# Q/K stacks loaded by sixteen rows: a new partition order and a second scratch tensor for the last four features

## The chip, the core and the metric

The kernel runs on one core of a Trainium2 chip. Its engines are TensorE (PE; its weight loads are listed apart as PEld), VectorE (DVE), ScalarE (ACT), GpSimd (POOL) and SyncE (SP). In this kernel SP issues all data transfers; 16 DMA engines carry them out. The metric is device time in microseconds of one launch, lower is better. Before the change three runs took 1097.66, 1098.9 and 1102.91 us, so the median is 1098.9 us.

## The reference

One transformer block in float32 on x of 2048 tokens by 640 features: sliding-window attention, then a gated MLP that mixes tokens. Only the first half matters for the change:

```python
B, S, D = x.shape
H = 32; Dh = D // H; W = 256                      # 32 heads of 20 features
qkv = (x @ wqkv).reshape(B, S, 3, H, Dh).transpose(2, 0, 3, 1, 4)
q, k, v = qkv
scores = einsum("bhqd,bhkd->bhqk", q, k) * Dh ** -0.5
mask = (i - j >= 0) & (i - j < W)                 # causal, 256 wide
p = softmax(where(mask, scores, -1e9))
o = einsum("bhqk,bhkd->bhqd", p, v)
h = x + merge_heads(o) @ wo                       # x here is layer-normed before wqkv
h2 = h + gated_mlp(layernorm(h))                  # gelu, token mixing by a 2048 x 2048 matrix, w_out
```

## The kernel before, in words

**Split operands.** Q and K are kept to nearly float32 precision as sums of three bfloat16 parts (part 0 the largest). A score q·k is then a sum of six products of parts: (1,0), (0,1), (0,0), (0,2), (2,0), (1,1) as (Q part, K part). The kernel stacks these six along the contraction: one bfloat16 matmul over 6 x 20 = 120 partitions makes a whole score. Such an operand is called a stack. Three more partitions (120 to 122) carry the row maxima against ones, so that the score comes out with its maximum subtracted.

**Making the parts.** Ten weight tiles m = 0 to 9 of 128 columns give Q and K transposed; tiles 0 to 4 hold the first sixteen heads and 5 to 9 the others, and within five tiles the 640 columns are ordered by (Q or K, feature, head), 8 rows of features by 16 heads in a tile. `qk_item(m, c)` (15 matmuls) makes tile m for 512 tokens (chunk c); `split_qk` turns the result into three bfloat16 parts in a tile `sg` (VectorE, ScalarE and GpSimd in turn; three buffers), and SP stores it to a scratch tensor `qk_d` in HBM with one transfer of 384 KB (L650). Items run in the order n = 0 to 23 (tiles 0 to 5, pairs of tiles, chunks 0 to 3 within a pair), then sixteen "dense" items for tiles 6 to 9 that are mixed into the first scores.

**Loading the stacks.** The heads come in eight groups g of four. `load_stack(g)` (L343) reads a group's rows from `qk_d` into one of three slots: two tiles st[0], st[1] for the first and the second 1024 tokens (b), each with Q and K side by side (a = 0 and 1). For each of the six pairs j it moves the 20 rows of one part to every sixth partition, j, j + 6, ...; 2 x 6 x 2 = 24 transfers of 20 rows by 8 KB. It is a generator: each `next` issues one transfer, and the callers set how many go out at each step.

**Where the loads stand.** All transfers are queued on SP in the order of the program, and SP issues them in that order, each after the waits it needs. Group 0 is loaded during items n = 16 to 21, three transfers an item, and one transfer for each of the first score units; group 1 during the dense items, three each from n = 7. From there on the main loop has steps s = 0 to 129: at step s unit s (a group and a block of 128 keys: scores, exp on ScalarE, masks on GpSimd, product with V) and the maximum pass of unit s + 18 (`max_item`, VectorE). Group g of 2 to 7 is loaded during the sixteen steps from s = 16(g - 2), one or two a step; it is first used by the maximum pass fourteen steps after its first transfer.

**What a transfer waits for.** The compiler gives the transfers eight completion semaphores in rotation (DMAHW0 to DMAHW7 in the listings below), so each transfer on SP waits until the one eight places before it has landed. PE, DVE, ACT and POOL follow the written order as well around these places (L612 to L614 are the matmuls of `qk_item`, L377 the matmuls of the first eighteen maximum units, L373 of the others, L426 the scores, L454 the product with V; L630 to L645 are the steps of `split_qk`; L606 loads a row of scales `std`, L570 a weight tile `wqraw`).

## Time and profile before

| | before |
|---|---|
| median of three runs | 1098.9 us |
| the profiled execution's own time | 1096.99 us |
| its span, first to last instruction | 1095.3 us |
| PE busy | 1073.5 us, 98% |
| DVE, ACT, POOL busy | 779.6, 603.7, 308.9 us |
| data moved | 194.78 MB in 92293 packets |
| granted TensorE clock | 1.000 |

The profile is of one execution. The span lies inside the execution's own time; 1.7 us are around it. The stages that the change touches lie between about 146 us (first load of group 0) and about 410 us (last load of group 7). In a timeline row the first number is the start, the second the length; "SPq" is SP issuing a transfer, whose length is the issue alone and not the movement of the data. "[0.28 <-X]" is idle time of the engine before the row and what ended it; "issue" there means that the engine waited for nothing that the profile shows.

### The profile page before, as it was taken

The page shows a single profiled execution, that of the slowest core. Times are in us where ns is not written, and L with a number is a line of the kernel's source. Part 1 is how long each engine was busy: PE and PEld are TensorE (multiplying, and loading weights), DVE is VectorE, ACT ScalarE, POOL GpSimd, SP SyncE. Part 2 cuts the span into 40 slices and gives each one's busy share as a digit, 9 for nine tenths or more (in the row PEclk, how much of TensorE's full clock was granted, in tenths as well). Part 3 has the DMA queues.
Part 4 walks back from the last instruction along what each step waited for, and adds up shares of the span by engine and source line. Part 5 has one row for each costly group of instructions (what it writes and reads, how often), then busy time and mean ns, then how long its engine had stood idle before and what let it go on. Part 6 is the DMA issues. An engine that isn't in the chain of part 4 may idle for free.

```text
span 1095.3 us, 28703 instructions
## 1 busy us (share of the span) xinstructions
PE 1073.5 (98%) x11045; PEld 967.9 (88%) x11045; DVE 779.6 (71%) x2157; ACT 603.7 (55%) x1257; POOL 308.9 (28%) x446
## 2 busy tenths in 40 slices
PE   8999999999999999999999999999999999999998
PEld 8998886668888787699999998999999899999998
DVE  6643445779999997586677678656556899988674
ACT  4444433249989899766766557433358433333331
POOL 4414445668766677622200012000001000000000
PEclk9999999999999999999999999999999999999999
DMA  7834566465665565679845342242341567684542
GB/s 257 296 117 118 174 212 217 150 214 174 191 186 184 187 192 172 193 217 289 316 179 186 113 135 77 71 142 87 126 150 51 176 230 249 231 280 139 181 156 97
DMA packets 92293, 194.78 MB, mean 178 GB/s; under 512 B 11958, under 2 KB 46278, under 8 KB 88262
## 3 DMA queue, kind: packets, MB, share of 16 engines
q1 hardware_dynamic: 92156, 192.95, 54.0%
q8 instruction: 87, 1.43, 0.5%
q14 instruction: 50, 0.41, 0.1%
HBM read 127.90 MB, written 64.95 MB: 176 GB/s over the span
## 4 chain that ended last, share of the span: by engine, by line
PE 84%; DMA 4%; issue 4%; ACT 3%; DVE 2%; POOL 1%; SPq 1%; ACTq 0%; POOLq 0%; DVEq 0%
PE g L1217 23%; PE zb L1102 8%; PE pv L454 7%; PE bank L373 5%; PE bank L426 5%; PE qk L612 4%; PE qk L613 4%; PE qk L614 4%; PE out_x L1381 3%; PE zx L1042 2%; PE out_v L1381 2%; PE zv L1042 2%; PE zy L1042 1%; PE zw L1042 1%; PE bank L377 1%
## 5 line engine op out<-in xcount | busy, mean ns | idle before, releaser
L429 ACT ACTIVATE pt<-bank 128x384 f32<-128x384 f32 (+1 forms) x452 | 180.5, 486 | 14.5 <-PE bank L426 9.7
L1217 PE MATMUL g<-zl,aw 128*128 128x432 f32 x768 | 168.9, 357 | 1.0 <-ACT zl L864 1.0
L383 DVE CUSTOM_DVE_ANT_0 junk<-bank,strip 128x288 bf16<-128x288 f32 x392 | 155.8, 452 | 9.8 <-PE bank L373 5.6
L864 ACT ACTIVATE aw<-fx 128x512 fp32r<-128x512 f32 (+2 forms) x152 | 86.1, 587 | 128.4 <-DVE fx L858 53.6
L1217 PEld LDWEIGHTS g<-zl,aw 128*128 128x128 f32 x768 | 144.0, 188 | 7.4 <-ACT zl L864 1.4
L858 DVE TENSOR_TENSOR aw<-fx,aw 128x512 fp32r<-128x512 f32 (+2 forms) x152 | 95.7, 638 | 58.8 <-ACT aw L864 53.8
L454 PE MATMUL pv<-pt,v_sb 128*32 128x192 f32 (+3 forms) x1984 | 133.3, 322 | 2.9 <-POOL pt L433 1.2
L1217 PE MATMUL g<-ze,aw 128*128 128x432 f32 x576 | 132.6, 359 | 2.3 <-DVE row L858 2.3
L1217 PEld LDWEIGHTS g<-ze,aw 128*128 128x128 f32 x576 | 107.1, 188 | 9.0 <-DVE row L858 3.7
L433 POOL TENSOR_SCALAR_AFFINE_SELECT pt<-pt 128x512 f32<-128x512 f32 x128 | 82.6, 646 | 58.1 <-ACT pt L429 55.1
L426 PE MATMUL bank<-slot 123*32 123x288 bf16 (+8 forms) x1296 | 94.8, 273 | 1.0 <-ACT pt L429 0.6
L373 PE MATMUL bank<-slot 120*32 120x288 bf16 (+4 forms) x1248 | 91.6, 275 | 3.0 <-issue 2.8
L454 PEld LDWEIGHTS pv<-pt,v_sb 128*32 128x32 f32 x1984 | 64.1, 110 | 10.2 <-POOL pt L433 5.1
L436 POOL TENSOR_SCALAR_AFFINE_SELECT pt<-pt 128x512 f32<-128x512 f32 x112 | 71.0, 634 | 0.0
L426 PEld LDWEIGHTS <-slot 123*32 123x32 bf16 x1728 | 59.3, 96 | 11.5 <-issue 1.7
L858 DVE TENSOR_TENSOR row<-g,row 128x432 f32<-128x432 f32 x80 | 48.3, 603 | 21.3 <-PE g L1217 20.9
L373 PEld LDWEIGHTS <-slot 120*32 120x32 bf16 x1408 | 51.0, 95 | 14.0 <-issue 5.6
L383 DVE CUSTOM_DVE_ANT_0 junk<-bank,mask 128x384 bf16<-128x384 f32 (+2 forms) x120 | 51.4, 444 | 16.6 <-PE bank L377 14.7
L645 POOL TENSOR_TENSOR sg<-rest,sg 128x512 bf16<-128x512 f32 x39 | 45.6, 1169 | 57.7 <-ACT sg L644 45.2
L630 DVE TENSOR_TENSOR rest<-qk,std 128x512 f32<-128x512 f32 x36 | 24.8, 690 | 42.4 <-PE qk L614 41.2
L635 ACT ACTIVATE sg<-rest 128x512 bf16<-128x512 f32 x39 | 24.6, 631 | 54.1 <-DVE rest L630 52.3
L118 PE MATMUL wo_ps<-xb,xb 128*128 128x320 f32 x260 | 52.4, 311 | 0.5 <-DVE mvc L1496 0.5
(289 smaller groups left out, 2534.5 us busy)
## 6 DMA issues: line engine op xcount, KB each, us to landing
slot<-qk_d SPq DMA_DIRECT2D x144, 160.0 KB
fx<-wsp_in SPq DMA_DIRECT2D x32, 512.0 KB
qk_d<-sg SPq DMA_DIRECT2D x39, 384.0 KB
o_d<-ot SPq DMA_DIRECT2D x64, 128.0 KB
xb<-qk_d SPq DMA_DIRECT2D x48, 160.0 KB
fx<-hn_d SPq DMA_DIRECT2D x24, 320.0 KB
z_d<-row SPq DMA_DIRECT2D x16, 432.0 KB
g_d<-row SPq DMA_DIRECT2D x16, 432.0 KB
```

Source lines behind the costliest of these rows:

```text
L373: nc.tensor.matmul(ps[32 * j:32 * j + 32, o:o + w], one(st, 120, 0, hh, q0, 32), k, start=True, stop=True, tile_position=(0, 32 * j))
L383: nc.vector.tensor_tensor_reduce(out=junk[:, :n], in0=ps[:, :n], in1=keep, scale=1.0, scalar=NEG, op0=OP.add, op1=OP.max, accum_out=m_cols ...
L426: nc.tensor.matmul(ps[32 * i:32 * i + 32, b + o:b + o + w], one(st, 123, 1, hh, k0, 32), q, start=True, stop=True, tile_position=(0, 32 * i))
L429: nc.scalar.activation(pt[:, hh, :n], ps[:, :n], AF.Exp, scale=SCALE)
L433: nc.gpsimd.affine_select(out=pt[:, :, :P], in_=pt[:, :, :P], pattern=[[0, 4], [1, P]], base=0, channel_multiplier=-1, compare_op=OP.is_ge ...
L436: nc.gpsimd.affine_select(out=pt[:, :, 256:], in_=pt[:, :, 256:], pattern=[[0, 4], [-1, P]], base=-1, channel_multiplier=1, compare_op=OP. ...
L454: nc.tensor.matmul(ps[32 * hh:32 * hh + 32, a - 512 * c:b - 512 * c], v_sb[:, kb, v0:v0 + 32], pt[:, hh, a - kb * P:b - kb * P], start=fir ...
L858: (eng or nc.vector).tensor_tensor(out=out, in0=a, in1=b, op=op)
L864: nc.scalar.activation(out, a, AF.Copy)
L1042: nc.tensor.matmul(ps, a[x], b[:, y], start=start and m + x + y == 0, stop=stop and m == n - 1 and x == 1, skip_group_check=True)
L1102: nc.tensor.matmul(b[0][:, :HF], a[:, x, kk], win2[0][:, y, kk, h * HF:(h + 1) * HF], start=kk + x + y == 0, stop=kk == KD - 1 and x == 1)
L1217: nc.tensor.matmul(ps, w[m][:, x, k], zc[k][m][:, y], start=start and k + x + y == 0, stop=stop and k == 3 and x == 1, skip_group_check=True)
```

## The change

The stacks get another order of partitions. Pair j now lies seven partitions apart, j, j + 7, ..., for the first sixteen features; every seventh row (6, 13, ..., 111) and the last eight rows (112 to 119) hold the last four features, 24 rows of (pair, feature). The host orders the weight columns to match: tiles 0, 1 hold Q and tiles 2, 3 K for features 0 to 15, tile 4 the last four features of Q and then of K (the same for tiles 5 to 9).

`qk_d` keeps the first sixteen features alone. A new scratch tensor `qr_d` holds the last four features already repeated for the six pairs. So tiles 4 and 9 are stored by six transfers a chunk rather than one: for Q and for K, each part goes to all pairs that use it (three, two and one copies; the source is repeated by a zero step). A stack is loaded by 32 transfers rather than 24: 24 of 16 rows, and for each (b, a) one of 16 and one of 8 rows from `qr_d`. The bytes of a stack stay the same; the stores of tiles 4 and 9 double from 384 to 768 KB.

The pace of the generators follows: four loads an item for n = 16 to 22 (28 of the 32 of group 0), with the four from `qr_d` for the first token half last among these; four rather than three for group 1; two a step (three at some early steps of group 2) in the main loop.

```diff
@@ -49,7 +49,9 @@
     const = pool(ctx, "const")
     dram = pool(ctx, "dram", space=DRAM)
 
-    qk_d = dram.tile([2, 3, 2, 2 * DH, H // 2, S // 4], F32, name="qk_d")
+    qk_d = dram.tile([2, 2, 3, 2, 16, H // 2, S // 4], F32, name="qk_d")
+    qr_d = dram.tile([2, 2, 2, 6, DH - 16, H // 2, S // 4], F32, name="qr_d")
+    PAIRS = ((1, 0), (0, 1), (0, 0), (0, 2), (2, 0), (1, 1))
     m_d = dram.tile([8, 2, 3, 32, 64], F32, name="m_d")
     o_d = dram.tile([H, 32, S], F32, name="o_d")
     wo_d = dram.tile([KD, 2, P, D], F32, name="wo_d")
@@ -334,13 +336,19 @@
                 for h, ones in zip(st, slot_w[0]):
                     nc.sync.dma_start(h[120:123, 1], ones[120:123, 1])
                     yield
-            parts = ((0, 0), (0, 1), (0, 2), (1, 0), (1, 1), (2, 0))
-            loads = [(b, j, a) for b in range(2) for j in range(6) for a in range(2)]
+            q, heads = g // 4, slice(g % 4 * 4, g % 4 * 4 + 4)
+            loads = []
+            for b in range(2):
+                for j, parts in enumerate(PAIRS):
+                    for a in range(2):
+                        loads.append((st[b][j:j + 106:7, a], qk_d[q, a, parts[a], b, :, heads]))
+                for a in range(2):
+                    last = qr_d[q, a, b, :, :, heads].rearrange("j d h t -> (j d) h t")
+                    loads += [(st[b][6:112:7, a], last[:16]), (st[b][112:6 * DH, a], last[16:])]
             if g == 0:
-                loads.sort(key=lambda load: load[2])
-            for b, j, a in loads:
-                src = qk_d[g // 4, parts[j][a], b, a * DH:(a + 1) * DH, g % 4 * 4:g % 4 * 4 + 4]
-                nc.sync.dma_start(st[b][j:6 * DH:6, a], src)
+                loads = loads[:12] + loads[16:28] + loads[12:16] + loads[28:]
+            for out, src in loads:
+                nc.sync.dma_start(out, src)
                 yield
 
         def tokens(st, rows, a, hh, t0, n):
@@ -645,10 +653,21 @@
                 nc.gpsimd.tensor_tensor(out=sg[:, 2, :], in0=rest, in1=sg[:, 1, :], op=OP.subtract)
                 if final:
                     yield
-                T = S // 4
-                base = qk_d[m // 5, 0, c // 2, m % 5 * 8, 0, c % 2 * 256:c % 2 * 256 + 256]
-                nc.sync.dma_start(bass.AP(tensor=base.tensor, offset=base.offset,
-                                          ap=[[T, P], [2 * 2 * DH * H // 2 * T, 3], [1, 256]]), sg.bitcast(F32))
+                T, n, part = S // 4, H // 2, sg.bitcast(F32)
+                b, t = c // 2, slice(c % 2 * 256, c % 2 * 256 + 256)
+                if m % 5 < 4:
+                    base = qk_d[m // 5, m % 5 // 2, 0, b, m % 5 % 2 * 8, 0, t]
+                    nc.sync.dma_start(bass.AP(tensor=base.tensor, offset=base.offset,
+                                              ap=[[T, P], [2 * 16 * n * T, 3], [1, 256]]), part)
+                    return
+                for a in range(2):
+                    for p in range(3):
+                        js = [j for j, x in enumerate(PAIRS) if x[a] == p]
+                        base = qr_d[m // 5, a, b, js[0], 0, 0, t]
+                        step = (js[-1] - js[0]) // max(1, len(js) - 1)
+                        nc.sync.dma_start(bass.AP(tensor=base.tensor, offset=base.offset,
+                                                  ap=[[T, 64], [4 * n * T * step, len(js)], [1, 256]]),
+                                          part[64 * a:64 * a + 64, p:p + 1].to_broadcast([64, len(js), 256]))
 
             halves = [slice(0, HD), slice(HD, D)]
             load_x(0)
@@ -746,9 +765,9 @@
                     load_wqk(2 * q + 4 + r % 2)
                 for _ in qk_item(2 * q + r % 2, r // 2):
                     pass
-                if 16 <= n < 22:
-                    for _ in range(3):
-                        next(ld0, None)
+                if 16 <= n < 23:
+                    for _ in range(4):
+                        next(ld0)
 
             def dense_tail():
                 split_wqk(8)
@@ -762,7 +781,7 @@
                         s1 = pool(x01, "slot1p", side="right")
                         add_slot(1, [s1.tile([P, 2 * S], F32R, name=f"slot1_{i}") for i in range(2)])
                     if n >= 7:
-                        for _ in range(3):
+                        for _ in range(4):
                             next(ld1, None)
 
             pool_order.enter_context(tc.manual_schedule(engines={mybir.EngineType.Pool}))
@@ -787,8 +806,9 @@
         early, pre_ps = None, []
         for s in range(NU + 2):
             if s % NT == 0 and s < 6 * NT:
+                assert s == 0 or next(ld, 0) == 0
                 ld = load_stack(s // NT + 2)
-            for _ in range(1 + s % 2 if s >= NT else 2 * (s > 1)):
+            for _ in range(2 if s >= NT else (2 + (s % 2 == 0 and s < 14)) * (s > 1)):
                 next(ld, None)
             u1 = s + LEAD
             if s in (3, 4, 7, 10, 12):
@@ -1584,7 +1604,9 @@
     c = np.ascontiguousarray
     x = np.asarray(A_x)[0]
     w = np.asarray(A_wqkv).reshape(D, 3, H, DH)
-    wqk = w[:, :2].reshape(D, 2, 2, H // 2, DH).transpose(2, 1, 4, 0, 3).reshape(2 * D // P, 8, KD, P, H // 2)
+    wqk = w[:, :2].reshape(D, 2, 2, H // 2, DH).transpose(2, 1, 4, 0, 3)
+    wqk = np.concatenate([wqk[:, a, d] for d in (slice(0, 16), slice(16, DH)) for a in range(2)], axis=1)
+    wqk = wqk.reshape(2 * D // P, 8, KD, P, H // 2)
     wqk = wqk.transpose(0, 3, 2, 1, 4).reshape(2 * D // P, P, KD, P)
     wv = w[:, 2].reshape(D, D)
     wo = np.asarray(A_wo).reshape(H, KD, 4, D).transpose(1, 2, 0, 3).reshape(D, D)
```

The order of the instructions on PE, DVE, ACT and POOL is the same before and after; SP's changes. The first place is the end of the items n = 20 to 22 on SP, ahead of the first maximum pass. Before (`slot_0_102` is st[0] of group 0, `sg_2` and `sg_3` are chunks 2 and 3, L650 the stores):

```order
L570 DMA wqraw_1597<-wqk_in 128x640
L650 DMA qk_d<-sg_2_1591 128x3x256
L343 DMA slot_0_102<-qk_d 20x2048 x3
L606 DMA std_0_1626<-rstd_d 128x512
L650 DMA qk_d<-sg_2_1620 128x3x256
L650 DMA qk_d<-sg_3_1649 128x3x256
L606 DMA std_1_1684<-rstd_d 128x512
```

The three loads after the store of item 20 are the last that the first maximum pass needs; nothing of the stack stands behind item 21's store. After the change the same place, with the waits (`slot_0_103` is st[0], `slot_1_104` st[1], the lines are those of the new file; the six stores of item 20 begin four rows above):

```order
L668 DMA qr_d<-sg_2_1606 64x2x256 [waits DMAHW6_49]
L668 DMA qr_d<-sg_2_1606 64x256 [waits DMAHW7_49]
L351 DMA slot_1_104<-qk_d 16x2048 [waits DMAHW0_49]
L351 DMA slot_1_104<-qk_d 16x2048 [waits DMAHW1_49]
L351 DMA slot_1_104<-qk_d 16x2048 [waits DMAHW2_49]
L351 DMA slot_1_104<-qk_d 16x2048 [waits DMAHW3_49]
L614 DMA std_0_1648<-rstd_d 128x512 [waits DMAHW4_49,DVE_49]
L660 DMA qk_d<-sg_2_1641 128x3x256 [waits DMAHW5_49,Pool_49]
L351 DMA slot_0_103<-qr_d 16x2048 [waits DMAHW6_49]
L351 DMA slot_0_103<-qr_d 8x2048 [waits DMAHW7_49]
L351 DMA slot_0_103<-qr_d 16x2048 [waits DMAHW0_49]
L351 DMA slot_0_103<-qr_d 8x2048 [waits DMAHW1_49]
```

The last four loads that the first maximum pass needs have moved one item later, behind item 21's store, and each waits for the transfer eight rows above it, two of which are stores of item 20.

The second place is PE at the first maximum pass, the weight load that waits for the stack. Before:

```order
L613 MATMUL qk_0_1710<-xa,wqh_1535 128x512
L614 MATMUL qk_0_1710<-xa,wql_1536 128x512 [waits Pool_49]
L377 LDWEIGHTS slot_0_102 [waits DMAHW5_49,DMAHW4_49,DMAHW6_49,DMAHW2_49,DMAHW7_49,DMAHW1_49,DMAHW0_49]
L377 MATMUL bank_128<-slot_0_102 128x128
L612 MATMUL qk_0_1710<-xa,wqh_1535 128x512
```

`qk_0_1710` is the dense item of tile 7, chunk 0, whose matmuls stand around it. After (L385 and L620 to L622 are L377 and L612 to L614 in the new file):

```order
L621 MATMUL qk_0_1741<-xa,wqh_1544 128x512
L622 MATMUL qk_0_1741<-xa,wql_1545 128x512 [waits Pool_49]
L385 LDWEIGHTS slot_0_103 [waits DMAHW5_49,DMAHW6_49,DMAHW4_49,DMAHW7_49,DMAHW1_49,DMAHW0_49]
L385 MATMUL bank_129<-slot_0_103 128x128 [waits DMAHW1_49]
L620 MATMUL qk_0_1741<-xa,wqh_1544 128x512
```

Its place among PE's instructions has not moved; what it waits for now includes the four loads from `qr_d`, and the matmul itself waits for the last of them.

## The prediction

> **What bounds the kernel now.** I read the page first, then the busy times by stage, then what PE waited for, and last SP's timeline at the places where loads moved. The page and the stages:
>
> ```profile
> span 1095.3 us, 28703 instructions
> PE 1073.5 (98%) x11045; PEld 967.9 (88%) x11045; DVE 779.6 (71%) x2157; ACT 603.7 (55%) x1257; POOL 308.9 (28%) x446
> ```
> ```profile
> 0.00:240.00 240.00, 236.80 (x1263) 192.75 (x1264) 130.22 (x325) 95.07 (x164) 112.37 (x111) 1.00 0.60 196
> 240.00:440.00 200.00, 193.44 (x5823) 163.10 (x5822) 182.93 (x929) 185.47 (x482) 142.89 (x247) 1.00 0.59 183
> 440.00:1095.00 655.00, 643.22 (x3968) 612.04 (x3960) 466.49 (x906) 323.20 (x614) 53.62 (x90) 1.00 0.51 170
> ```
>
> The columns are the stretch, its length, PE, PEld, DVE, ACT and POOL busy, clock, DMA share, GB/s. PE is busy throughout. The change touches 146 to 410 us, and there PE is idle for no more than the 200 − 193.4 = 6.6 us of the attention stage. So a gain has a small ceiling; a loss has none, since every microsecond that PE waits for a stack is added to the end: the instructions of PE follow a written order. What that idle time waited for, from 240 to 440 us (us in total, times, longest):
>
> ```profile
> PE bank L373 <- issue: 3.4, 5, 1.6
> PE pv L454 <- issue: 1.1, 3, 0.6
> PE bank L426 <- ACT pt L429: 0.9, 6, 0.2
> PE bank L426 <- issue: 0.3, 1, 0.3
> ```
>
> Nothing of it is put down to a stack load. 3.4 + 1.1 + 0.3 = 4.8 us have no cause that the profile shows. All transfers go through SP:
>
> ```profile
> slot<-qk_d SPq DMA_DIRECT2D x144, 160.0 KB
> qk_d<-sg SPq DMA_DIRECT2D x39, 384.0 KB
> std<-rstd_d SPq DMA_DIRECT2D x15, 256.0 KB
> wqraw<-wqk_in SPq DMA_DIRECT2D x10, 320.0 KB
> ```
>
> **What an issue costs on SP.** Lengths in ns are lowest/median/highest:
>
> ```profile
> L343 SPq DMA_DIRECT2D slot<-qk_d x144: 694/722/1977, 145.9 to 409.7; - x144
> L525 SPq DMA_DIRECT2D rstd_d<-std_row x1: 336/336/336, 73.6 to 73.6; - x1
> L400 SPq DMA_DIRECT2D slot<-m_d x12: 266/271/442, 215.0 to 438.1; - x12
> L650 SPq DMA_DIRECT2D qk_d<-sg x39: 359/366/414, 92.9 to 239.6; - x39
> ```
>
> A load of 20 rows takes 0.72 us to issue. No row of before shows one of 16 or 8 rows out of HBM into a slot. The nearest by its rows is the store of 16 rows, 0.34 us, and the load of 3 rows into the same slot takes 0.27; so neither the row count nor the 8 KB rows explain the 0.72, and I take 0.34 for all the new loads. The bounds are 0.27 and 0.72. A six-part store is six issues of 0.37, 2.2 us for 0.37 before. SP keeps about 0.06 us between issues.
>
> [...]
>
> **The place that decides: group 0 before the first maximum pass.** SP around it, and PE:
>
> ```profile
> 149.51 0.39 SPq L650 DMA_DIRECT2D qk_d<-sg  x1
> ...
> 164.60 0.38 SPq L650 DMA_DIRECT2D qk_d<-sg  x1
> 165.03 2.41 SPq L343 DMA_DIRECT2D slot<-qk_d  x3
> 167.54 0.41 SPq L606 DMA_DIRECT2D std<-rstd_d  x1
> 168.21 2.16 SPq L650 DMA_DIRECT2D qk_d<-sg  x2
> ```
> ```profile
> 173.14 0.40 PE L614 MATMUL qk<-xa,wql 128*128 128x512 f32 x1
> 173.38 0.23 PE L377 MATMUL bank<-slot 120*128 120x128 bf16 x1
> ```
> ```profile
> L377 PEldq EVENT_SEMAPHORE  x3: 51/51/51, 171.9 to 172.8; - x3
> ```
>
> The first row is the store of item 16, 164.60 that of item 20, 165.03 the last loads that the first maximum pass needs; the pass starts at 173.38 right behind a matmul. The last row is PE's sequencer asking for the stack's semaphores: 51 ns each, so nothing was waited for and all had landed by 172.8. The stack was ready some 5 us after its last issue (167.4), with at most a little to spare.
>
> After the change the last four loads stand behind item 21's store, which waits for GpSimd until 168.2. At 0.40 us a piece (0.34 and the gap) they are issued by 168.2 + 0.4 + 4 x 0.40 = 170.2 at the earliest. A transfer's landing on a quieter queue is bounded here:
>
> ```profile
> 173.29 0.69 DVE L630 TENSOR_TENSOR rest<-qk,std 128x512 f32<-128x512 f32 x1 [1.25 <-DMA std<-rstd_d]
> 170.46 0.49 SPq L606 DMA_DIRECT2D std<-rstd_d  x1
> ```
>
> At most 2.8 us from issue to use, if that wait is for this transfer; then the four loads are there at 173.0 and nothing is lost. That is the lower end. But the DMA queue is not quiet:
>
> ```profile
> 150.00:155.00 5.00, 5.00 (x23) 4.02 (x22) 2.04 (x3) 2.33 (x4) 2.70 (x2) 1.00 0.75 220
> 155.00:160.00 5.00, 5.00 (x23) 4.03 (x22) 2.08 (x3) 1.81 (x4) 2.34 (x2) 1.00 0.72 262
> 160.00:165.00 5.00, 5.00 (x23) 3.98 (x23) 2.08 (x3) 1.99 (x4) 1.17 (x1) 1.00 0.93 295
> 165.00:170.00 5.00, 5.00 (x23) 4.03 (x22) 1.95 (x3) 2.42 (x5) 2.37 (x3) 1.00 0.97 314
> ```
>
> The last columns: the DMA engines go from 75% to 97% busy. What has to land between item 16's store and the last needed load: before, 5 stores of 384, 15 loads of 160, 2 std of 256 and 2 wqraw of 320 KB, 5.6 MB. After: three six-part stores of 768, three stores of 384 (items 17, 19, 21), 20 loads of 128, the four late ones (384 together), 3 std, 2 wqraw, 8.0 MB. At the rate that the busiest rows give when full, 314/0.97 = 324 GB/s, 8.0 MB take 24.7 us; with 2 us until the first lands (2.8 us less the 0.8 us in which 256 KB move at 324) that is 149.5 + 2.0 + 24.7 = 176.2. The rows 155 to 160 give 262/0.72 = 364 GB/s and 173.5. Near the end the rate of the fullest row counts, so I take 176.2: PE waits 176.2 − 173.2 = **3.0 us**. With eight completion semaphores and transfers half the size, SP cannot run ahead of this either: the last load waits for one of item 21's loads, that one for a transfer before item 20's store. If issue stays at 0.72 it is worse (a rival, below). Queued behind the waiting weight load are all of PE's dense matmuls; DVE's maxima and `split_qk` wait for those, and the later stages follow. Nothing behind it makes the time good: PE is busy for 5.00 of 5.00 us in each of these rows, and in the attention stage it is idle for 3%.
>
> [...]
>
> **The other parts.** The six-part stores hold their `sg` buffer longer. ACT waits for one of three already:
>
> ```profile
>   ACT sg L635: 0.3, 1
> ```
>
> At 2 us more it is ACT and GpSimd that run later, beside a `rest` buffer that PE's result does not need for two further items; I cost it at nothing, and up to 1 us if that cover goes. The stores of tile 9 stand among the dense items and at step 12, with group 4 as the first reader thirty steps later: nothing. In the main loop SP's loads cost 2 x 0.40 us a step instead of 1.5 x 0.78, and even at 0.78 they would be 1.6 us of a step of 1.7, as the scores show (128 units from 237.0 to 456.2):
>
> ```profile
> L426 PEld LDWEIGHTS <-slot x1728: 92/97/101, 237.0 to 456.2; 123*32 123x32 bf16 x192
> ```
>
> The first half of a stack is complete after 16/2 = 8 steps as after 12/1.5 = 8 before, six steps ahead of its use. The rows of the new order cost PE the same, 120 partitions. So the handovers of groups 1 to 7 cost nothing.
>
> What can be gained is in the 4.8 us without a cause. The longest of them falls on a time of slow issues:
>
> ```profile
> 304.35 5.01 SPq L343 DMA_DIRECT2D slot<-qk_d  x5
> 308.09 0.24 PE L373 MATMUL bank<-slot 120*32 120x192 bf16 x1 [1.60 <-issue]
> q8 instruction: 87, 1.43, 0.5%
> ```
>
> Five loads took 1.0 us each, and instructions come over DMA too, so a crowded queue may be behind it. The bytes of the loads stay the same; bounds 0 and 4.8 us, and I take 0.7, below the middle because a cause is not shown.
>
> **The sum.** +3.0 − 0.7 = +2.3 us on a span of 1095.3, so 1097.6, and 1099.3 for that execution's own time of 1096.99. The median of before, 1098.9, is 1.9 above that execution; on the same footing I predict **1101 us**, 0.2% more.
>
> **The rivals.** About 0.5% (5.5 us) is what a measurement of this kernel can tell from no change.
> *Hidden.* The four late loads land by 173.2, as the 2.8 us and the 364 GB/s allow, and only the 0.7 us show: 1098.2. For it: PE's semaphores were satisfied without a wait. Against it: 2.4 MB more in the same stretch.
> *SP falls behind (slower).* 16 rows still cost 0.72. Two items then take 7 store issues of 0.43, 8 loads of 0.78, one std of 0.47: 9.7 us, where four items take the 15.1 us from 149.51 to 164.60, 7.5 for two. SP loses 2.2 us a pair, 6.6 over three, so the last load is issued at 168.6 + 6.6 + 4 x 0.78 = 178.3 and lands at 181.1; PE waits 8 us: 1106. It decides from an issue of 0.44 us on, where 3.0 + 8 x 0.50 + 0.47 us reach the 7.5. Against it: the 16-row store at 0.34.
> *The crowd clears (faster).* The attention stage's 4.8 us vanish and nothing is late: 1094.1, still inside 0.5%. For it: the slow issues at 304 us. Against it: such waits stand also where no stack is loaded (PE is idle 11.8 us after 440).
>
> **How the numbers follow.** Forecast 0.53, hidden 0.27, SP falls behind 0.14, the crowd clears 0.06. The forecast's own range is 1098 to 1105: a stall of 0.3 to 3.0 by the two rates, up to 6 if landing is slower under load. The range to 8 in 10 reaches down into the hidden case with 4 of the 4.8 us gained (1094.9) and up past the slower rival's 1106: 1095 to 1107. Slower by over 0.5% (over 1104.4): the rival and 0.07 of the forecast, 0.21. Faster by over 0.5% (under 1093.4): 0.05, the tail of the last case. Within: 0.74.
>
> **What would show it.** In the profile after: a wait of PE or PEld on L385 for a load from `qr_d` at about 173 us, near 3 us (0 for hidden, 8 for the rival); issue of the 16-row loads near 0.34 us; DMA share at 0.95 or more from 155 to 175; waits on "issue" of 240 to 440 us at about 4. It would be wrong if the loss came elsewhere, say at a later group's first use, or if attention got faster by more than its idle time.

## The result and the profile after

The changed kernel takes 1134.7 us in the median (1129.1 to 1137.0, six runs) against 1098.8 for the kernel before on the same chip (1097.5 to 1102.9, six runs): a ratio of 1.030, with a 95% interval of 1.0277 to 1.0325. It is 36 us slower; I had predicted 1101 us, 2 us slower, and a range that ended at 1107. The profiled execution of the changed kernel took 1129.1 us, so what the trace shows is 32 us of it. The head of its page:

```profile
span 1127.3 us, 28869 instructions
PE 1080.7 (96%) x11045; PEld 971.2 (86%) x11045; DVE 781.2 (69%) x2157; ACT 605.0 (54%) x1257; POOL 311.3 (28%) x446
```

PE executes the same 11045 matmuls in the same order as before, so the start times of equal matmuls can be subtracted, and the difference grows exactly where time is lost. It grows to 13.9 us until 188.7 us, stays there to the end of the dense stage, grows by another 18 us through the attention stage (279 to 453 us), and stays at 32 us to the end. The same in the stages, with the columns of the prediction's table (stretch, length, PE, PEld, DVE, ACT, POOL busy, clock, DMA share, GB/s):

```profile
0.00:254.00 254.00, 239.13 (x1263) 193.87 (x1264) 130.75 (x323) 95.02 (x164) 111.90 (x111) 0.97 0.64 194
254.00:470.00 216.00, 196.50 (x5771) 164.04 (x5775) 183.97 (x929) 184.46 (x478) 142.44 (x244) 0.98 0.61 172
470.00:1127.00 657.00, 645.07 (x4020) 613.30 (x4012) 466.51 (x907) 325.52 (x617) 56.93 (x93) 1.00 0.51 170
```

The first row holds the 1263 matmuls that ended at 240 us before: 14 us longer, of which 11.7 are idle time of PE (254 − 239.1 = 14.9 us against 240 − 236.8 = 3.2) and 2.3 are PE busy longer. The attention row has 19.5 us of idle PE against 6.6. The idle time was waited for on these (us in total, times, longest):

```profile
PE bank L385 <- DMA slot<-qr_d: 7.7, 1, 7.7
PE bank L381 <- DMA slot<-qr_d: 6.0, 3, 2.9
PE qk L620 <- DVE rest L638: 3.3, 1, 3.3
PE bank L381 <- DMA xb<-qr_d: 3.2, 2, 1.9
PE bank L381 <- DMA slot<-qk_d: 2.0, 1, 2.0
```

The first is the wait at the first maximum pass, which I had forecast at 3.0 us. The second, fourth and fifth are handovers, the places where PE first uses one half of a later group's stack; I had costed them at nothing. The third lies ahead of the first: PE's dense matmuls wait for a `rest` buffer whose `sg` has not been stored yet. SP around the first maximum pass (start, length of the run of issues, how many):

```profile
171.78 4.33 SPq L668 DMA_DIRECT2D qr_d<-sg  x6
176.16 2.71 SPq L351 DMA_DIRECT2D slot<-qk_d  x4
178.98 0.52 SPq L614 DMA_DIRECT2D std<-rstd_d  x1
179.59 0.38 SPq L660 DMA_DIRECT2D qk_d<-sg  x1
180.02 2.27 SPq L351 DMA_DIRECT2D slot<-qr_d  x4
```

Each row begins where the one above ends: SP is never free, and its last needed issue ends at 182.3, not at 170.2 as I had worked out. The pass starts at 186.1:

```profile
186.08 0.29 PE L385 MATMUL bank<-slot 120*128 120x128 bf16 x1 [7.67 <-DMA slot<-qr_d]
```

What SP's issues cost (ns, lowest/median/highest):

```profile
L351 SPq DMA_DIRECT2D slot<-qk_d x144: 484/587/1692, 146.0 to 441.1; - x144
L351 SPq DMA_DIRECT2D slot<-qr_d x48: 378/485/1710, 180.0 to 445.4; - x48
L668 SPq DMA_DIRECT2D qr_d<-sg x42: 468/605/2004, 148.6 to 245.4; - x42
```

In the median a load of 16 rows takes 0.587 us to issue, one of the last rows 0.485, and each of the six stores of a tile's last features 0.605. I had 0.34, 0.34 and 0.37. The rest of this text is about whether this is the cause, why those prices were wrong, and why the attention stage could not bear them.

### The profile page after: what moved, and what is told of

It reads as the page before. It is cut to its first block, busy times and chain, and to the rows that moved or that the text cites. A ratio compares the mean times of both kernels' runs of the same rounds, so it can differ in the third digit from the quotient of the medians.

```text
span 1127.3 us, 28869 instructions
## 1 busy us (share of the span) xinstructions
PE 1080.7 (96%) x11045; PEld 971.2 (86%) x11045; DVE 781.2 (69%) x2157; ACT 605.0 (54%) x1257; POOL 311.3 (28%) x446
## 4 chain that ended last, share of the span: by engine, by line
PE 71%; DMA 10%; ACT 6%; issue 5%; DVE 4%; SPq 2%; POOL 2%; POOLq 0%; ACTq 0%; DVEq 0%
PE g L1237 22%; PE pv L462 4%; PE zb L1122 4%; PE qk L620 4%; PE qk L622 3%; PE qk L621 3%; PE bank L381 3%; PE bank L434 3%; PE out_x L1401 3%; PE zx L1062 2%; ACT pt L437 2%; PE out_v L1401 2%; PE zv L1062 2%; DMA m_d<-m 1%; PE zy L1062 1%
## 5 line engine op out<-in xcount | busy, mean ns | idle before, releaser
L434 PE MATMUL bank<-slot 123*32 123x288 bf16 (+7 forms) x1296 | 96.2, 274 | 1.3 <-ACT pt L437 0.6
```

Of the source, the lines that this page charges most:

```text
L434: nc.tensor.matmul(ps[32 * i:32 * i + 32, b + o:b + o + w], one(st, 123, 1, hh, k0, 32), q, start=True, stop=True, tile_position=(0, 32 * i))
```

## The experiments

Kernels that alter the changed kernel are shown as a diff against it, the others against the kernel before. The diffs are cut to the lines that matter: `...` stands for what is left out of a line, and lines that only follow from the ones shown are missing.

**What an issue costs.** A program without the computation (it only copies the input to the output) issues series of loads and stores of the forms in question.

```diff
+ load(20, 6)  x8   # rows, partition step
+ load(16, 7)  x8
+ load(16, 1)  x8
+ load(8, 1)   x8
+ load(24, 1)  x8
+ load(120, 1), load(128, 1), load(32, 1)  x4 each
+ load(16, 7) of half the length, load(16, 1) contiguous in memory, load(3, 1)  x8 each
+ stores of 128 x 3 x 256, 64 x 3 x 256 (one part repeated, or three parts), 64 x 256  x6 each
```

> This program computes nothing of the reference but copies x to the output: it only queues transfers on SP, one form after another, to price their issue alone: loads of 20 rows six partitions apart, of 16 rows seven apart and next to each other, of 8, 24, 120, 128, 32 and 3 rows, 16 rows of half the length, 16 and 3 rows that lie next to each other in HBM, 16 and 20 rows one at a time, and the stores of 128x3x256, 64x3x256 repeated and not, and 64x256. Theory (a price per form): 20 rows cost 0.72 us as in the kernel, 16 rows 0.48 alone and 0.59 behind another, whatever their stride, and the parts stores 0.5 to 0.6 for half the rows of a 0.37 store. Rival (a crowded chip): with nothing else running 16 rows cost 0.34 us, like the store of 16 rows that I took for them, and the 0.59 in the changed kernel came from the traffic around.

The rows of the line that issues, each in the window of one series: 20 rows six apart, 16 rows seven apart, then 16, 8 and 24 rows on neighbouring partitions:

```profile
L44 SPq DMA_DIRECT2D big<-wsp_in x7: 715/715/724, 1.7 to 6.3; - x7
L44 SPq DMA_DIRECT2D big<-wsp_in x8: 581/587/587, 7.7 to 12.1; - x8
L44 SPq DMA_DIRECT2D big<-wsp_in x6: 409/418/418, 12.7 to 15.0; - x6
L44 SPq DMA_DIRECT2D big<-wsp_in x7: 272/272/272, 18.6 to 25.5; - x7
L44 SPq DMA_DIRECT2D big<-wsp_in x8: 297/298/298, 26.7 to 34.6; - x8
```

The program has nothing else to do, and the prices of the loads are those of the two kernels: 0.72 and 0.59 us. So they are no effect of a crowded chip. The step between partitions counts, which I had expected not to matter: 16 rows cost 0.587 seven apart and 0.418 as neighbours, each right behind another issue, and 0.505 and 0.311 alone (after a pause of SP). The last two rows above are of issues alone, and so are 0.24 for 3 neighbouring rows and 0.31 to 0.36 for 32, 120 and 128: among neighbours the row count hardly counts. Rows of half the length cost the same 0.505 as whole ones, seven apart and alone, so it isn't the bytes either.

Two more things set the price. With spread rows their number counts: the run without the last features, below, loads 16 rows six apart where the kernel before loads 20 six apart, and its median is 0.58 instead of 0.72:

```profile
L345 SPq DMA_DIRECT2D slot<-qk_d x144: 484/582/1770, 145.7 to 408.4; - x144
```

And an issue is dearer behind a dear one. The 8 neighbouring rows of the changed kernel, which cost 0.272 alone here, cost 0.48 in the median there, each right behind a load of 16 spread rows. So a form has no price of its own, and I don't know how the time is shared out between two issues. A store from 64 partitions took 0.60 with one run of 256 a partition and 0.9 with three; the stores' prices don't carry over as the loads' do, since one from 128 partitions took 0.37 alone in the kernel before and up to 1.2 behind others here.

**Without the last features.** The kernel before with loads of 16 rows instead of 20; features 16 to 19 of Q and K are left out of the scores, and with them the six-part stores and the loads of the last rows.

```diff
-                src = qk_d[g // 4, parts[j][a], b, a * DH:(a + 1) * DH, ...]
-                nc.sync.dma_start(st[b][j:6 * DH:6, a], src)
+                src = qk_d[g // 4, parts[j][a], b, a * DH:a * DH + 16, ...]
+                nc.sync.dma_start(st[b][j:j + 91:6, a], src)
```

> The kernel before, with 16 rather than 20 rows in each of its 24 loads a group (same stride, same pace, stores as before); features 16 to 19 are left out of the scores, their rows hold ones. Theory (SP's issue time): 24 issues of 0.63 us rather than 0.76, so SP is freer than before, no stack is late and the time is that of the kernel before or up to 4 us less. [...]

1099.98 us against 1100.63 for the kernel before: a ratio of 0.9992 (0.997 to 1.0013). Loads of 16 rows by themselves bring nothing and, in sum, cost nothing. The loss comes with what the change does for the four features that are left. This doesn't clear the 16-row loads of a part in it, as SP's account below shows.

**The dense stage: number or bytes of the stores.** Two kernels store four copies of the largest part alone for Q and for K, so that the scores of the last features are computed from wrong parts. One writes them by one store a side, two a chunk; the other writes the same bytes by three stores a side, six a chunk as in the change.

```diff
-                    for p in range(3):
-                        js = [j for j, x in enumerate(PAIRS) if x[a] == p]
+                    for j0, cnt in ((0, 4),):                    # two stores a chunk
+                    for j0, cnt in ((0, 2), (2, 1), (3, 1)):     # six stores a chunk
```

> The changed kernel with the last features' rows stored by two transfers a chunk (four copies of the largest part, one transfer for Q and one for K; 512 KB) rather than six (768 KB); all pairs read those copies, so the scores are not the reference's. Loads as in the changed kernel. Theory (SP's issue time): six issues of 0.63 us become two, 2.5 us less for each of the three stores ahead of the first maximum pass, so its delay falls from 12.7 us to about 5, and the total from 32 us over the kernel before to about 24; the 18 us of the attention stage stay. Rival (bytes): the delay falls too, but then six stores of the same 512 KB do the same.

> As the kernel with two stores, but the same 512 KB in six transfers a chunk (2, 1 and 1 copies for Q and for K). Theory (SP's issue time): the delay at the first maximum pass is that of the changed kernel, 11 to 13 us. Rival (bytes): it is that of the kernel with two stores, 5 us or less.

Two stores: 1126.4 us, ratio 1.022 (1.0187 to 1.0253), and the first maximum pass is 6.9 us late instead of 12.7. Six stores with the same bytes: 1137.0 in one run, the pass 11.5 us late. SP's timeline of each around that place, first of the kernel with two:

```profile
167.82 1.35 SPq L666 DMA_DIRECT2D qr_d<-sg  x2
169.74 2.93 SPq L351 DMA_DIRECT2D slot<-qk_d  x4
```

and of the one with six:

```profile
170.77 4.27 SPq L666 DMA_DIRECT2D qr_d<-sg  x6
175.08 2.49 SPq L351 DMA_DIRECT2D slot<-qk_d  x4
```

So the number of stores makes most of it and what they carry little: with the same bytes six stores rather than two cost 4.6 us at the pass, and half as many bytes again, in the changed kernel, 1.2 us more. A third test has the stores and (for groups 2 to 7) the loads of the last rows issued from POOL's queue, with the same transfers as in the change:

```diff
-                nc.sync.dma_start(out, src)
+                (nc.gpsimd if g > 1 and k % 16 > 11 else nc.sync).dma_start(out, src)
...
-                        nc.sync.dma_start(bass.AP(tensor=base.tensor, ...
+                        nc.gpsimd.dma_start(bass.AP(tensor=base.tensor, ...
```

> As the run with the last features' loads on POOL's queue, and the stores of six parts issued from POOL's queue too. Theory (SP's full queue makes both losses): SP is rid of 84 stores of 0.6 us, 42 of them in the stretch where the first maximum pass waits; the dense stage's 14 us should fall to what the first groups' own loads cost, 3 to 6 us, and the total come to 1100 to 1110 us, if POOL's issues do not delay its own tiles: in the dense stage POOL is busy 18 of 45 us from 145 to 190, so there is room for some 25 us of issuing. Rival (the stores' bytes and landing times make the dense loss, whoever issues them): the dense loss stays at 10 us or more, total within 4 us of the run with the loads alone.

1124.0 us, ratio 1.0219 (1.0185 to 1.0253). The first maximum pass is 5.8 us late instead of 12.7, since SP now comes to the last needed loads 8.2 us earlier:

```profile
169.55 0.53 SPq L614 DMA_DIRECT2D std<-rstd_d  x1
171.23 0.38 SPq L660 DMA_DIRECT2D qk_d<-sg  x1
171.78 3.92 SPq L351 DMA_DIRECT2D slot<-qr_d  x4
```

The stores' bytes are the same, and the dense stage loses 7 us up to 227 us instead of 14, so the rival for this stage (bytes and landing, whoever issues) fell there. In the four kernels the pass starts 3.5 to 4.3 us after SP's last needed issue has ended, however late that is. The total missed: I had expected 1100 to 1110 us, and with 3 us between this run and the next it lies where the rival had put it. (I had counted 84 stores; there are 48, and 18 of them stand ahead of the last load that the first maximum pass needs.) The later part of this run is no clean test, as the run with only the loads moved shows (the first line of the diff alone):

> The changed kernel with the last features' loads (8 of 32 a group) issued from POOL's queue instead of SP's in the groups 2 to 7; the same transfers, the same stores, the first two groups as they were. Theory (SP's full queue makes the loss in attention): 48 issues of 0.485 us and their gaps, some 27 us, leave SP, which then has standing time again as in the kernel before; attention's 18 us should fall to 0 to 5 us, the dense stage's 14 us stay, total 1111 to 1119 us, unless POOL, which is busy for 64 to 70 percent of that stage, is held by issuing: then PE's waits for POOL's tiles grow from 1 to 5 us or more. Rival (the transfers of the last rows themselves, their traffic on the engines, make the loss): above 1125 us as before.

1127.0 us, ratio 1.0244 (1.0217 to 1.0271): the total is where the rival had put it, above 1125, but by way of the exception that I had named for my own theory. In the attention stage PE no longer waits for stacks; it now waits for POOL's work, which stands behind the issues there, and where the profile shows no cause:

```profile
PE pv L462 <- POOL pt L441: 8.8, 13, 1.7
PE bank L381 <- issue: 4.1, 3, 3.2
```

The wait for `pt` was 1.2 us before. An issue took 0.518 to 0.537 us of POOL, 25 us for the 48, on an engine that has its own place in every step. The price moved with the issue: the handover waits went with SP's load, but the attention stage still loses 15 us, so this run doesn't tell whether SP alone was the cause.

**The attention stage: SP's time alone.** The kernel before, its loads and stores untouched, gets tiny stores (8 rows of 128, 4 KB) on SP's queue in groups 2 to 7: 12 a group, and then 4 a group.

```diff
                 nc.sync.dma_start(st[b][j:6 * DH:6, a], src)
+                if g > 1 and a:                  # 12 a group; for 4: and j % 3 == 0
+                    more[0] += 1
+                    nc.sync.dma_start(extra_d[more[0] % 16], ident[:8])
```

> The kernel before with its loads and stores as they were, and 12 small stores of 8 rows by 128 added on SP's queue in each of the groups 2 to 7, one ahead of every second load: 72 issues of about 0.3 us, 22 us in all, which bring SP's sum of issue time in that stretch from 140 to some 162 us of 170, where the changed kernel has 159 of 187. Their bytes are negligible (4 KB each). Theory (SP's occupancy alone makes the loss in attention): SP falls behind there too, PE waits for stacks at the group changes, and the kernel is slower by 5 to 20 us (1104 to 1119), with PE waiting for qk loads at the end of the groups. Rival (the layout of the changed kernel's loads, or the fetches that hold them, make the loss): within 0.5 percent of the kernel before, since the loads themselves are unchanged.

> The kernel before with 4 instead of 12 of the small stores (8 rows by 128) in each of the groups 2 to 7: 24 issues of about 0.27 us, with their gaps some 8 us of SP's time. Theory (a full queue: SP's own account): of the 155 us from 255 to 410 of the kernel before, SP issues for 129.5 us, spends 12.9 us on gaps between issues and semaphore reads, and stands for 13.1 us, 8.1 of them waiting for the store of the maxima to land. So 8 us added find 5 to 13 us of standing time: the kernel should be slower by 0 to 3 us only (1099 to 1104). With 12 stores a group, 21 us added made it 23 us slower. Rival (each added issue delays PE by its own length, wherever it stands): a third of 23 us, 7 to 8 us (1107 to 1109).

With 12 a group: 1122.3 us against 1101.2, ratio 1.0192 (1.0154 to 1.0229). With 4: 1110.2 against 1100.6, ratio 1.0081 (1.005 to 1.0113). The issues and what PE waited for, with 12:

```profile
L347 SPq DMA_DIRECT2D extra_d<-ident x72: 280/458/1261, 245.8 to 437.5; - x72
```
```profile
PE bank L377 <- DMA slot<-qk_d: 6.5, 6, 1.9
PE bank L377 <- DMA xb<-qk_d: 4.0, 2, 2.3
PE bank L377 <- DMA o_d<-ot: 3.0, 1, 3.0
PE bank L377 <- DMA extra_d<-ident: 2.5, 1, 2.5
```

These are the handover waits of the changed kernel, made by issues that carry next to nothing. The loss is 21.0 us for 72 issues and 9.6 for 24, 0.29 and 0.40 us for each, against the 0.46 us that one takes. My figure of 13 us of standing time was no reserve: the rival of the smaller test held, and the loss is even above its 7 to 8 us. I summed SP's time in the trace from 255 to 410 us of the kernel before, and in the others between the same two matmuls of PE:

| us | before | changed | 12 more | 4 more | no last features |
|---|---|---|---|---|---|
| stretch | 155 | 173 | 173 | 168 | 155 |
| issues | 199 | 247 | 255 | 219 | 203 |
| their time | 129.5 | 147.9 | 151.7 | 138.0 | 124.7 |
| of it, issues over 0.8 us: number, time above the median of their form | 14, 7.6 | 27, 19.1 | 11, 6.4 | 12, 7.5 | 28, 19.2 |
| gaps between them, semaphore reads | 12.9 | 15.2 | 16.1 | 14.4 | 12.8 |
| standing over 0.12 us at a time | 13.1 | 10.0 | 5.3 | 15.7 | 17.6 |

Before, 142.4 of 155 us were taken, and 11.6 of the 13.1 us of standing were waits for the store of the maxima (`m_d`) to land, during which nothing behind it in the queue can go. The changed kernel adds 18.4 us of issue time and 2.3 us of gaps, and the stretch is 18 us longer. With 12 more, SP stands for less time than before, so the loss there isn't made of waits for landings.

The fourth row shows what I had overlooked. Of the 18.4 us only 6.9 are issues at their ordinary price; 11.5 come from 27 long issues where there were 14. The run without the last features has the same long issues, but its ordinary ones are 16.4 us cheaper, so SP is freer in sum and nothing is lost. The long issues come with loads of 16 rows: 22 to 30 over this work in each of eight kernels that have them, 9 to 14 in four with 20 rows. The tests with added issues show that more SP time is enough to make such a loss; that the long issues make over half of it in the changed kernel is read from these sums, and no run took them away alone.

**Cheaper issues.** If the partition step makes the price, neighbouring partitions should mend it. First the changed kernel with 16 neighbouring partitions a load:

```diff
-                        loads.append((st[b][j:j + 106:7, a], ...
+                        loads.append((st[b][16 * j:16 * j + 16, a], ...
-                    loads += [(st[b][6:112:7, a], last[:16]), ...
+                    loads += [(st[b][96:112, a], last[:16]), ...
```

> The changed kernel with one thing altered: each pair's 16 rows go to 16 neighbouring partitions (16j to 16j+15) instead of every seventh one, and the last 24 rows to partitions 96 to 111 and 112 to 119. The same 32 loads a group, the same bytes, the same number of rows a load, the same stores of six parts. Theory (the partition stride sets the price of an issue, and SP's occupancy makes the loss): 16 neighbouring rows took 0.42 us behind another load against 0.59 with the stride, so the mean issue of a pair's load should fall from 0.587 to about 0.42 us and that of the last rows from 0.485 to 0.3 to 0.4 us; a group's 32 loads then take some 13 us instead of 18, SP has idle time again in the attention stage, and of its 18 us nearly all should vanish. The dense stage keeps its 42 part stores of 0.605 us, and its loss of 14 us falls only by what the first group's loads cost less, to some 10 to 12 us. Total about 1110 us (1107 to 1115). [...] A second rival: neighbouring partitions are written more slowly, the loads land later, and PE waits at the first maximum pass as long as before or longer.

then the kernel before with 20:

```diff
-                nc.sync.dma_start(st[b][j:6 * DH:6, a], src)
+                nc.sync.dma_start(st[b][DH * j:DH * j + DH, a], src)
```

> The kernel before with one thing altered: each pair's 20 rows go to 20 neighbouring partitions (20j to 20j+19) instead of every sixth one; the same 24 loads a group and the same stores. Theory (partition stride sets the price): the issue of a load falls from 0.72 us to 0.3 to 0.45 us, SP's sum of issue time in the stretch of loads falls from 140 to some 90 us. Since SP already had idle time in the kernel before, and PE is busy 98 percent of the time, the total is within 0.5 percent of it, at best 4 us less (1095 to 1100). [...] Second rival (neighbouring partitions are written more slowly): issues are cheap, but loads land later and PE waits longer for the stacks.

The first took 1170.0 us, ratio 1.0629 (1.0594 to 1.0664) to the kernel before, the second 1127.7, ratio 1.0248 (1.0212 to 1.0283). The prices fell as expected; the times rose, as the second rival said. From the first:

```profile
L351 SPq DMA_DIRECT2D slot<-qk_d x144: 302/418/1692, 146.3 to 471.9; - x144
```
```profile
PE bank L434 <- issue: 17.7, 10, 4.5
PE bank L381 <- issue: 13.0, 7, 3.6
PE bank L385 <- DMA qr_d<-sg: 10.6, 1, 10.6
```

and of the queue of all transfers from 280 us on (packets, MB, share of 16 engines' time), from 280 to 460 us of the first, and from 280 to 420 us of the changed kernel:

```profile
q1 hardware_dynamic: 12571, 26.43, 85.7%
```
```profile
q1 hardware_dynamic: 10963, 22.66, 57.6%
```

A packet held its engine for 0.857 x 16 x 180 / 12571 = 196 ns on average, against 0.576 x 16 x 140 / 10963 = 118 ns with the partitions seven apart; the 8-KB packets of the loads alone took 732 against 474 ns in the mean of the attention stage. The DMA engines are 86% busy, and PE waits where the profile shows no cause, up to 4.5 us at a time. In the kernel with 20 neighbouring partitions SP stood for 36 us waiting for the store of the maxima to land (17 before):

```profile
SPq L400 <- DMA m_d<-m: 35.7, 15, 4.5
```

So the spread of the partitions, which makes the issue dear (0.587 against 0.418 us in the median), goes with faster transfers (474 against 732 ns a packet). What slows the packets on neighbouring partitions no run shows.

**One load fewer a side.** The changed kernel with the last 24 rows on partitions 96 to 119 by one load, the others six apart: 28 loads a group instead of 32.

```diff
-                        loads.append((st[b][j:j + 106:7, a], ...
+                        loads.append((st[b][j:j + 91:6, a], ...
-                    loads += [(st[b][6:112:7, a], last[:16]), (st[b][112:6 * DH, a], last[16:])]
+                    loads.append((st[b][96:6 * DH, a], last))
```

> The changed kernel with the last features' 24 rows on neighbouring partitions (96 to 119), fetched by one load instead of two, and the other 16 rows six partitions apart instead of seven: 28 loads a group instead of 32. The stores of six parts stay. Theory (SP's occupancy): four issues a group fewer and four others cheaper save 4 x 0.49 + 4 x 0.1 = 2.4 us of SP's 27 us a group, so the attention stage's loss falls from 18 us by 6 x 2.4 = 14 us at most, to 4 to 10 us; the dense stage's loss of 14 us falls by 1 to 2 us; total 1115 to 1124 us. [...]

1140.9 us in one run, not better than the change (1134.7): the expectation was wrong by 20 us. Long issues don't explain it: over the work of the table they are 22 rather than 27, and the issue time fell, to 130 us over 178. SP's waits for the store of the maxima grew instead, from 13.8 us in the whole changed kernel to 43.4, and PE now waits for the maxima:

```profile
SPq L408 <- DMA m_d<-m: 43.4, 15, 4.1
```

The same row of the changed kernel, and then what PE waited for in this one:

```profile
SPq L408 <- DMA m_d<-m: 13.8, 12, 2.9
```
```profile
PE bank L434 <- DMA slot<-m_d: 11.8, 4, 3.7
PE bank L385 <- DMA qr_d<-sg: 9.2, 1, 9.2
PE bank L434 <- DMA xb<-m_d: 4.2, 2, 2.2
```

In the changed kernel two loads of last rows are issued between the store of the maxima and the load that waits for it. Here two loads stand there in every other case and none in the rest, and SP stands for 2.4 to 4.2 us with them and 2.6 to 4.1 without (291 to 437 us). So the order doesn't explain it: the load of the maxima, which waits for the store to land, follows the store's issue after 3.6 to 6.2 us, in the changed kernel after 2.3 to 4.9. Why the store lands later stays open.

**Fewer, larger loads.** Last, a try for a kernel that beats both: the pairs in an order in which those that read the same part are neighbours, so that one load fills 60, 40 or 20 neighbouring partitions, 14 loads a group instead of 24.

```diff
-                nc.sync.dma_start(st[b][j:6 * DH:6, a], src)
+                src = bass.AP(tensor=src.tensor, offset=src.offset, ap=[[0, n], *src.ap])
+                nc.sync.dma_start(st[b][DH * j:DH * (j + n), a], src)
```

> The kernel before with fewer and larger loads of the same rows: the six pairs are put in the order (1,1), (1,0), (2,0), (0,0), (0,1), (0,2), each on 20 neighbouring partitions, so that pairs that read the same part follow one another and one load writes 60 (three pairs), 40 (two) or 20 partitions, reading the part's 20 rows repeatedly: 14 loads a group instead of 24, 3.8 MB a group as before, the stores as before. A load of three pairs counts as three in the pacing. Theory: SP's issue time is what the attention stage has least of (24 small issues more cost 9 us), and a load on neighbouring partitions is issued in 0.3 to 0.4 us whatever its rows; a group's issuing falls from 17 to 5 us, PE no longer waits for the loads, and the kernel reaches 1092 to 1099 us (PE's idle time in attention is some 6 us). Rival, from the run with 20 neighbouring partitions a load: transfers to neighbouring partitions are slower and come in bursts, the store of the maxima lands after 6 us instead of 4, instruction fetches and output stores wait behind them: slower by 10 to 30 us (1108 to 1130), as 20 partitions a load were (1127.7). [...]

1290.9 us, ratio 1.1728 (1.1693 to 1.1763): far beyond what either side had expected. PE waits for the loads, while the DMA engines are hardly used (the queue from 280 to 420 us):

```profile
PE bank L375 <- DMA slot<-qk_d: 70.6, 11, 11.0
PE bank L375 <- DMA xb<-qk_d: 38.0, 5, 9.2
```
```profile
q1 hardware_dynamic: 5465, 13.41, 29.4%
```

What makes these loads slow isn't shown: no run separates the repeated source from the neighbouring partitions. The price of an issue that I had expected was wrong too: a load of 60 neighbouring rows took 0.72 us, not 0.3 to 0.4, so neighbouring partitions with a repeated source aren't cheap. No kernel of this study beats the one before.

## Why the prediction was wrong

*The view and the place.* PE's written order, and that nothing behind a wait makes it good: right, the differences stay to the end. The place in the dense stage: right, PE waits on L385 for loads from `qr_d`. The other half of the loss came at "a later group's first use", which the prediction named as what would prove it wrong.

*The price of an issue.* This is the step that failed. I took 0.34 us for all new loads from a store of 16 rows on neighbouring partitions and excluded the row count on the strength of a 3-row load. Both rows had a partition step of one and nearly all stood behind a pause of SP; the loads they stood for are spread or stand behind spread ones. The row of the 3-row load could have told: its highest, 0.442, is the one issued right behind another load (at 215 us). And with spread rows the count matters: four rows fewer, six apart, cost 0.58 instead of 0.72. Measured for the new loads: 0.587 and 0.485. The bounds (0.27 and 0.72) held it, and the range should have gone by them: the rival "SP falls behind" was said to decide from 0.44 us on.

*The six-part store.* Six times 0.37 us was the price of a store from 128 partitions that stands alone; from 64, repeated and behind another, it was 0.605, and one chunk took SP 4.3 us instead of 2.6.

*The stall.* Forecast 3.0 us, by the rate of the DMA engines (landing at 176.2). Measured: the pass starts 12.7 us late, the dense stage loses 13.9 in all. It was SP that was late, with the last issue ending at 182.3 and 3.8 us from there to the pass; the runs with two and six stores show that the issues count far more than the bytes. With the measured prices the rival's own sum gives per two items one six-part store (4.33) and one plain (0.43), 8 loads of 0.63 and one `std` (0.57): 10.4 us for 7.5, so 8.6 us lost over three pairs and the last issue at 168.6 + 8.6 + 4 x 0.57 = 179.5. That is 3 us short of 182.3, and near it.

*Buffers.* "ACT and GpSimd run later, up to 1 us": PE itself waited 3.3 us for `rest`, ahead of the pass.

*The handovers of groups 1 to 7.* Costed at nothing, measured at 18 us, the largest error. I had set two loads of 0.78 us against a step of 1.7 us and found 1.6 small enough. The sum left out what else SP does in a step: output stores, maxima, gaps, and the waits for landing, which left 1 to 2 us of 155 that were really free. The tests with added issues show that there was hardly any cover. It left out the long issues too, over half of what SP had more to do.

*The gain of 0.7 us from quieter queues.* Nothing of it. Waits on "issue" aren't among the large ones after, but issues got slower rather than faster: the trace has 30 of 265 issues over 0.8 us (253 to 440 us) against 14 of 217 before (240 to 410), and 27 of the 30 overlap a fetch of instructions. So do 43 of the 235 shorter ones, and 13 of the 14 before, so a fetch alone doesn't make an issue long. In the run without the last features there are as many, and no time is lost, since its other issues are cheaper.

*The rivals.* The slower one had the right mechanism, a chance of 0.14, and less than a quarter of the size (8 of 36 us): it was worked out for the dense stage alone. Its condition, an issue over 0.44 us, held with 0.587. "Hidden" and "the crowd clears" fell with the pass 12.7 us late.

## What to carry to other kernels

Before more transfers are put on a queue, add up everything that the issuing engine does in the stage, gaps and waits for landings included, and not only the transfers that change: here 142 of 155 us were taken, and each further issue of 0.46 us cost 0.3 to 0.4 us of the kernel's time. A price of an issue may be borrowed only from a row with the same step between partitions (16 rows took 0.59 us seven apart and 0.42 as neighbours), about as many rows (0.72 for 20 and 0.58 for 16, six apart) and the same kind of issue ahead of it (8 rows took 0.27 alone and 0.48 behind 16 spread ones). And a cheaper issue isn't a gain by itself: neighbouring partitions cut it by 29 and 53% and made two kernels 3.2 and 2.5% slower than the same with spread ones, while the transfers themselves slowed down (in the first a packet held its engine for 196 ns on average, against 118).

## What the runs showed that I had not expected

The time that SP takes to issue a load depends on the step between its partitions (behind another, 0.59 us for 16 rows seven apart and 0.42 for neighbours) and, for neighbours, hardly on the number of rows (alone, 0.27 to 0.36 us for 8 to 128); for spread rows it does depend on it (0.72 us for 20 and 0.58 for 16, six apart). It depends on the issue ahead as well: 8 neighbouring rows took 0.27 us alone and 0.48 behind 16 spread ones.

PE also ran slower after some of its waits. Stretches around the late first pass and a late handover of the changed kernel, with the granted clock as the third number from the right:

```profile
170.00:180.00 10.00, 5.74 (x18) 4.30 (x18) 2.87 (x4) 3.26 (x5) 4.15 (x3) 0.83 0.96 293
180.00:190.00 10.00, 3.92 (x13) 2.37 (x14) 2.18 (x8) 1.89 (x3) 3.52 (x4) 0.66 0.79 216
290.00:300.00 10.00, 7.37 (x214) 6.07 (x206) 5.98 (x30) 5.46 (x14) 4.46 (x9) 0.83 0.62 163
```

The clock records have stretches at half speed of 3.41 us (once 6.83) after five of the waits, where the kernel before has none after 10.7 us, and PE is busy 7.2 us longer in all, a fifth of the loss, which I put down to them. What sets such a stretch off isn't shown: of the 3.4 us ahead of it PE was busy for 0.7 and 0.0 us at 172 and 182 us, and for 1.1 to 1.3 us at 295, 326 and 421 us, where its longest single waits were 1.3, 0.9 and 2.3 us.
